# A linear-attention and expert kernel on one core: an early indirect transfer, idle matmuls, one key decay moved, and second loads that wait

## The chip, the cores and the metric

The kernel runs on one core of one Trainium2 chip. The metric is the device time of one execution in microseconds (us); lower is better. The time before is the median of three runs. One further execution was taken with the hardware profiler, and all rows below come from it.

The core's engines run beside each other: PE (TensorE, matrix products; its weight loads are listed as PEld), DVE (VectorE), ACT (ScalarE), POOL (GpSimd) and SP (SyncE), which in this kernel issues nearly all transfers. POOL issues the indirect transfers, whose rows go where a list of numbers says.

## The reference

First a blocked linear attention with decay over q, k and v of shape (4, 8, 768, 64), then a mixture of eight experts of which each token uses one:

```python
for b in range(nb):                                   # 12 blocks of 64 positions
    intra = einsum('bhic,bhjc->bhij', qb, kb) * Dmask
    intra = einsum('bhij,bhjd->bhid', intra, vb)
    inter = einsum('bhid,bhde->bhie', qb * lam_pow, kv_state)
    out[:, :, sl] = intra + inter
    kv_state = lam_block * kv_state + einsum('bhsd,bhse->bhde', kb * rev_pow, vb)
...
x = attention.transpose(0, 2, 1, 3).reshape(3072, 512)
e_idx = argmax(x @ w_gate + modality_bias[modality_id], axis=1)
for e in range(8):
    mask = e_idx == e
    out[mask] = gate_w[mask, None] * (relu(x[mask] @ w1[e]) @ w2[e])
```

## The kernel before

The attention works in blocks of 128 positions: 24 blocks g, six for each of the four batches, two to a load. A pair of blocks is the unit of the main loop (m = 2 to 11); blocks 0 to 5 are written out ahead of it. For each block PE computes `scores(g)` (into a PSUM tile `s`), DVE multiplies them with the decays (`mask`, tile `pt`), PE multiplies with the values (`values`, tile `o`), and adds what comes from the running state (`from_state`, with the decayed queries `qd`, which POOL makes in `query`). `products(g)` multiplies the decayed keys `kd` with the values into PSUM tile `kv`, and `add` on DVE updates the state. The decayed keys are made in `keys`: on ACT in eight pieces (line 238), or on POOL in one instruction (line 234). `give` on ACT copies a finished `o` to `xt`; `turn` and `gates` turn it and compute the gate's logits.

From the middle of the attention on, tokens are sorted: DVE finds the expert and a slot for each token in small steps that `do` releases a few at a time, and POOL writes the rows into a DRAM table `placed` with indirect transfers (`one_slot`, line 433), one after the other, each held by `tick` until a certain matmul is done. After about 100 us the expert tiles follow: twelve wide tiles of 256 rows and two thin ones, each with weights that SP loads into buffers that the tile before has freed.

The order on PE, DVE, ACT and SP is the order of the code. POOL's order is too: `pool` chains its instructions in the order of its calls. Each engine therefore stands still behind an instruction that waits. The pairs of blocks lie in four buffers (`SLOTS`, tag `load`); in the main loop `load(m + SLOTS, [0])` fetches the first block of a later pair and, one pair on, `load(m + SLOTS - 1, [1])` the second block of that buffer.

`decays` and `powers` on DVE (lines 120 and 129) compute the decay tables `dk` and `pq` at the start, and `keep_busy(9)` issues nine bf16 matmuls on zeros, whose result nobody reads, before the first scores.

Of the kernel before, what the change touches and what calls it, by code (L numbers as in the profile page):

```python
# [6 lines left out]
F32 = mybir.dt.float32  # L7
F32R = mybir.dt.float32r
BF16 = mybir.dt.bfloat16
I32 = mybir.dt.int32  # L10
# [5 lines left out]
P = 128  # L16
# [4 lines left out]
SLOTS = 4  # L21
# [22 lines left out]
def linear_attention_moe(tc, qkv, lam, modality, wg, mbias, w1, w2, out):  # L44
    nc = tc.nc
    with ExitStack() as ctx:
        const = ctx.enter_context(tc.tile_pool(name="const", bufs=1))
        dram = ctx.enter_context(tc.tile_pool(name="dram", bufs=1, space=bass.MemoryType.DRAM))
# [12 lines left out]
        def pool(op, free=False):  # L61

            for first in queue[-1:] + ([] if free else loose):
                tc.add_manual_dep(op.ins, first.ins.name,
                                  mybir.DependencyInfo(mybir.DependencyClass.NoSync, mybir.DependencyReason.SCHED_ONLY),
                                  reason="order")
            if free:
                loose.append(op)
            else:
                loose.clear()  # L70
                queue.append(op)
            return op
# [4 lines left out]
        def slot(shape, dt, nm):  # L77

            return work.tile(shape, dt, name=nm, tag="load", bufs=SLOTS)

        def source(m):
            return qkv[divmod(m, NC // HB)].rearrange("x p c f -> p x c f")

        halves = {}

        def load(m, blocks=range(HB)):
            if m not in halves:
                halves[m] = slot([P, 4, HB, H * D], F32, "load")
            last = (HB * m + 1) % NC == NC - 1
            if m > 2 and not last and len(blocks) == HB:  # L90
                nc.sync.dma_start(out=halves[m], in_=source(m))
                return
            for c in blocks:
                for part in ((slice(0, 2), slice(2, 4)) if m < 2 else (slice(0, 4 - (last and c)),)):
                    nc.sync.dma_start(out=halves[m][:, part, c], in_=source(m)[:, part, c])

        for m in range(3):
            load(m)
# [3 lines left out]
        nought = const.tile([P, P], F32, name="nought")  # L102
# [5 lines left out]
        pool(nc.gpsimd.affine_select(out=anti, in_=anti, pattern=[[1, P]], compare_op=ALU.not_equal,  # L108
                                     fill=1.0, base=1 - P, channel_multiplier=1))

        dk = work.tile([P, 2, NP, P], F32, name="dk", bufs=1)
        pq = work.tile([P, NP, P], F32, name="pq", bufs=1)
        lamq = const.tile([P, NP], F32, name="lamq")
# [97 lines left out]
        def loaded(g):  # L211

            t = halves[g // HB][:, :, g % HB]
            kt, qt = (t[:, i].rearrange("p (a t) -> p a t", a=NP) for i in range(2))
            return kt, qt, t[:, 2], t[:, 3]
# [11 lines left out]
        def keys(g, on_pool=False):  # L227

            if g % NC < NC - 1:
                kds[g] = work.tile([P, NP, 2, D], F32, name="kd", bufs=3)  # L230
                kn = loaded(g)[3].rearrange("p (a h d) -> p a h d", a=NP, h=2)
                if on_pool:
                    last = dk[:, :, :, P - 1 : P].rearrange("p h a o -> p a h o").to_broadcast([P, NP, 2, D])
                    pool(nc.gpsimd.tensor_tensor(out=kds[g], in0=kn, in1=last, op=ALU.mult))
                    return
                for p in range(NP):
                    for hl in range(2):
                        nc.scalar.activation(out=kds[g][:, p, hl, :], in_=kn[:, p, hl, :], func=AF.Copy,  # L238
                                             scale=dk[:, hl, p, P - 1 : P])
# [5 lines left out]
        def after(op, mm):  # L245
            tc.add_manual_dep(op.ins, mm.ins.name,
                              mybir.DependencyInfo(mybir.DependencyClass.Sync, mybir.DependencyReason.DATA),
                              reason="order")
            return op

        def scores(g):
            kt, qt, vt, kn = loaded(g)
            scs[g] = ps.tile([P, 2, NP, P], F32, name="s", bufs=2)
            for p in range(NP):
                for hl, r in enumerate(halves2):
                    mm = nc.tensor.matmul(scs[g][:, hl, p, :], kt[r, p, :], qt[r, p, :], start=True, stop=True)  # L256
            begun[g] = mm
            return mm

        def mask(g):  # L260
            pts[g] = work.tile([P, 2, NP, P], F32, name="pt", bufs=4)
            nc.vector.tensor_tensor(out=pts[g], in0=scs.pop(g), in1=dk, op=ALU.mult)  # L262

        def products(g):

            if g % NC < NC - 1:
                vt, kd = loaded(g)[2], kds.pop(g)
                for p in range(NP):
                    for hl, r in enumerate(halves2):
                        nc.tensor.matmul(kp[r, g % HB, p, :], kd[:, p, hl, :],  # L270
                                         vt[:, (2 * p + hl) * D : (2 * p + hl + 1) * D], start=True, stop=True)
# [105 lines left out]
        def gate_rows():  # L377
            lgt = work.tile([P, RC, WG], F32, name="lgt", bufs=2)
            nc.vector.transpose(out=lgt, in_=lps.rearrange("p g (t a) -> p (g t) a", a=Q))
            return lgt  # L380
# [74 lines left out]
        def tick(mm):  # L455

            if jobs:
                after(jobs.pop(0)[1](), mm)
# [347 lines left out]
        def keep_busy(n):  # L806

            nothing = ps.tile([P, NP, P], F32, name="o", bufs=2).rearrange("p a t -> p (a t)")
            for i in range(n):
                nc.tensor.matmul(nothing, busy[:, :P], busy, start=(i == 0), stop=(i == n - 1))  # L810
# [13 lines left out]
        def block(g, on_pool=False):  # L824
            mm = scores(g)
            mask(g)
            keys(g, on_pool)
            query(g)
            return mm
# [5 lines left out]
        keys(0, True)  # L835
        scores(0)
        mask(0)
        scores(1)
        products(0)
        add(0)  # L840
# [1 line left out]
        mask(1)  # L842
        query(1)
        keys(1)
        keys(2)
        from_state((1,))
        values(1)
        scores(2)
# [39 lines left out]
        for m in range(2, pairs):  # L888
            a, b = HB * m, HB * m + 1
            ahead = m + 1 < pairs  # L890
            add(b)
            if m == 4 or m == 8:
                routed = m // 4 - 1, *choose(m // 4 - 1, gate_rows())
            if ahead:
                block(a + 2)
                mm = block(b + 2)
                if m > 4:
                    tick(mm)
                if 2 < m <= pairs - SLOTS:
                    load(m + SLOTS - 1, [1])  # L900
                if m == 9:
                    fetch_w1(*some, parts=range(2, 4))
                elif m == 10:
                    fetch_w2(*some, parts=range(2, 4))
            if m == 5 or m == 9:
                ranks(routed[-1])
                slots += slots_of(*routed)
            if m == 2:
                routing_constants()
            elif m == 3:  # L910
                clear(slice(E * CAP, E * CAP + TT), TT)
            do(9 if m % 4 == 0 else 8)
            if m == 2:
                mm = values(b, begins=True)
                from_state((a, b), ends=True)
            elif not ahead:
                values(a, begins=True)
                mm = values(b, begins=True)
                from_state((a, b), ends=True)
            else:  # L920
                from_state((a, b))
                values(a)
                mm = values(b)
            if m > 4:
                tick(mm)
            if m + SLOTS < pairs:
                load(m + SLOTS, [0])
            if ahead:
                products(a + 2)
                products(b + 2)  # L930
                add(a + 2)
            if m == 10:
                turn_rows(0)
            elif m % 2 and ahead:
                mm = turns(m // 2, begin_list)
                if m == 5 or m == 9:
                    jobs += [("slots", one_slot)] * RC
                if m > 4:
                    tick(mm)
            if m == 8:  # L940
                need("slots")
                raw1 = w1_part("raw1", F32)
                some = fetch_regs(0, True)
                fetch_w1(*some, parts=range(2))
                fetch_x(0)
            elif m == 9:
                raw2 = w2_part("raw2", F32)
                some = fetch_regs(0, True)
                fetch_w2(*some, parts=range(2))
                fetch_x(1)  # L950
# [97 lines left out]
        for n in [3] + list(range(wides, fixed_ones)):  # L1048
# [5 lines left out]
            m = n + 1 if n > 3 else wides  # L1054
# [91 lines left out]
```

## Time and profile before

| what | value |
|---|---|
| median of three runs | 393.74 us (393.1 to 394.73) |
| the profiled execution's own time | 393.09 us |
| its span, first to last instruction | 391.4 us |
| PE busy | 379.1 us (97%) |
| DVE, ACT, POOL busy | 261.2, 211.7, 96.3 us |
| mean granted clock of PE | 0.990 of full |

The profiled execution took 393.09 us, 0.65 us less than the median. 1.7 us of it lie outside the span. Busy time of PE counts matmuls from issue to a modelled end, so a busy PE may still run at half its clock; the granted clock has to be read beside it.

### The profile page before, as it was taken

How to read it: one execution, taken by the hardware profiler on the slowest of the kernel's cores; microseconds unless marked ns; L12 is line 12 of the kernel's file. 1: busy time of each engine (PE TensorE's matmuls, PEld its weight loads, DVE VectorE, ACT ScalarE, POOL GpSimd, SP SyncE). 2: the span in 40 equal slices, each digit the busy share in tenths (PEclk: the TensorE clock that was granted, in tenths of full speed). 3: DMA queues.
4: the chain of work that ended last, by engine and by line, in shares of the span. 5: the costliest groups of instructions: out<-in, count | busy, mean ns of one | idle time of the engine just before them, and what ended most of it. 6: DMA issues, size and time to landing. Idle time of an engine off the chain costs nothing.

```text
span 391.4 us, 9721 instructions
## 1 busy us (share of the span) xinstructions
PE 379.1 (97%) x3597; PEld 337.3 (86%) x3597; DVE 261.2 (67%) x461; ACT 211.7 (54%) x419; POOL 96.3 (25%) x127
## 2 busy tenths in 40 slices
PE   6999999899999999999999999999999999999994
PEld 3888988799888989989898987898979899898983
DVE  6468779988678578886758574376775756667520
ACT  1668578496446464465566444355454644655611
POOL 1365214865520267120010201202011020201112
PEclk9799999999999999999999999999999999999999
DMA  7999986986998994299813999663860211100101
GB/s 249 387 403 359 342 269 214 389 275 165 311 344 266 338 320 160 109 377 340 266 55 77 294 384 346 266 186 91 293 212 36 55 55 44 40 25 10 49 3 52
DMA packets 44568, 82.72 MB, mean 211 GB/s; under 512 B 7390, under 2 KB 20190, under 8 KB 44512
## 3 DMA queue, kind: packets, MB, share of 16 engines
q1 hardware_dynamic: 40592, 69.23, 53.1%
q0 software_dynamic: 3920, 12.78, 8.4%
q8 instruction: 30, 0.49, 0.6%
q14 instruction: 26, 0.21, 0.2%
HBM read 89.52 MB, written 17.84 MB: 274 GB/s over the span
## 4 chain that ended last, share of the span: by engine, by line
PE 39%; issue 33%; DMA 9%; DVE 7%; POOL 6%; ACT 3%; SPq 2%; POOLq 0%; DVEq 0%; ACTq 0%
DMA raw<-in_w_dram 5%; POOL out_dram L736 4%; PE o L692 4%; PE o L694 4%; PE o L693 4%; PE s L256 3%; PE o L313 3%; PE o L332 3%; PE s L694 2%; PE s L693 2%; PE s L692 2%; PE s L712 2%; PE kv L712 2%; DVE pt L262 2%; PE kv L692 2%
## 5 line engine op out<-in xcount | busy, mean ns | idle before, releaser
L601 DVE TENSOR_TENSOR w2l<-raw,w2h 128x1024 fp32r<-128x1024 f32 x48 | 58.8, 1224 | 37.5 <-ACT w2h L600 34.0
L736 POOL DMA_INDIRECT out_dram<-y,idx x24 | 29.6, 1232 | 213.8 <-ACT y L735 171.1
L692 PE MATMUL o<-w2h,hh 128*128 128x512 f32 x192 | 75.3, 392 | 0.0
L694 PE MATMUL o<-w2h,hl 128*128 128x512 f32 x192 | 74.8, 390 | 0.0
L693 PE MATMUL o<-w2l,hh 128*128 128x512 f32 x192 | 74.8, 389 | 0.0
L601 DVE TENSOR_TENSOR w1l<-raw,w1h 128x1024 fp32r<-128x1024 f32 x44 | 51.4, 1220 | 2.0 <-ACT w1h L600 2.0
L600 ACT CAST w2h<-raw 128x1024 fp32r<-128x1024 f32 x48 | 49.9, 1039 | 2.0 <-DMA raw<-in_w_dram 1.9
L692 PE MATMUL kv<-xh,w1h 128*128 128x256 f32 x176 | 49.6, 282 | 0.0
L692 PE MATMUL s<-xh,w1h 128*128 128x256 f32 x176 | 49.6, 282 | 0.0
L693 PE MATMUL s<-xl,w1h 128*128 128x256 f32 x176 | 49.5, 281 | 0.0
L693 PE MATMUL kv<-xl,w1h 128*128 128x256 f32 x176 | 49.5, 281 | 0.0
L694 PE MATMUL s<-xh,w1l 128*128 128x256 f32 x176 | 49.5, 281 | 0.0
L694 PE MATMUL kv<-xh,w1l 128*128 128x256 f32 x176 | 49.4, 281 | 0.0
L692 PEld LDWEIGHTS o<-w2h,hh 128*128 128x128 f32 x192 | 36.1, 188 | 7.9 <-issue 0.8
L600 ACT CAST w1h<-raw 128x1024 fp32r<-128x1024 f32 x44 | 42.8, 1045 | 0.0
L694 PEld LDWEIGHTS o<-w2h,hl 128*128 128x128 f32 x192 | 36.0, 188 | 7.6
L693 PEld LDWEIGHTS o<-w2l,hh 128*128 128x128 f32 x192 | 36.1, 188 | 7.1
L735 ACT ACTIVATE y<-o,idx 128x512 f32<-128x512 f32 x24 | 16.4, 684 | 41.1 <-PE o L694 38.3
L238 ACT ACTIVATE kd<-load,dk 128x64 f32<-128x64 f32 x152 | 37.6, 338 | 0.1
L692 PEld LDWEIGHTS kv<-xh,w1h 128*128 128x128 f32 x176 | 33.3, 189 | 0.4 <-issue 0.4
L692 PEld LDWEIGHTS s<-xh,w1h 128*128 128x128 f32 x176 | 33.2, 189 | 0.3
L693 PEld LDWEIGHTS s<-xl,w1h 128*128 128x128 f32 x176 | 33.2, 189 | 0.4
(190 smaller groups left out, 637.8 us busy)
## 6 DMA issues: line engine op xcount, KB each, us to landing
raw<-in_w_dram SPq DMA_DIRECT2D x96, 512.0 KB
load<-in_qkv_dram SPq DMA_DIRECT2D x12, 1024.0 KB
both<-in_w_dram SPq DMA_DIRECT2D x16, 512.0 KB
xg<-placed SPq DMA_DIRECT2D x48, 128.0 KB
placed<-blank SPq DMA_DIRECT2D x9, 528.0 KB
load<-in_qkv_dram SPq DMA_DIRECT2D x8, 512.0 KB
load<-in_qkv_dram SPq DMA_DIRECT2D x2, 2048.0 KB
load<-in_qkv_dram SPq DMA_DIRECT2D x4, 768.0 KB
```

The costliest lines, as they stand in the source:

```text
L238: nc.scalar.activation(out=kds[g][:, p, hl, :], in_=kn[:, p, hl, :], func=AF.Copy, scale=dk[:, hl, p, P - 1 : P])
L256: mm = nc.tensor.matmul(scs[g][:, hl, p, :], kt[r, p, :], qt[r, p, :], start=True, stop=True)
L313: mm = nc.tensor.matmul(op[place(g, hl), p, :], vt[:, (2 * p + hl) * D : (2 * p + hl + 1) * D], pt[:, hl, p, :], start=((begins or g % NC ...
L332: nc.tensor.transpose(out=tp[:, p, :], in_=xts[grp][:, p, tb].rearrange("k t a -> k (t a)"), identity=ident)
L600: nc.scalar.copy(out=hi, in_=src)
L601: nc.vector.tensor_tensor(out=lo, in0=src, in1=hi.bitcast(F32), op=ALU.subtract)
L692: nc.tensor.matmul(out, ah, bh, start=first, stop=False)
L693: nc.tensor.matmul(out, ah, bl, start=False, stop=False)
L694: return nc.tensor.matmul(out, al, bh, start=False, stop=last)
L712: mm = nc.tensor.matmul(hp[:, j, :], raw1[i][:, kc, fs], xt2[:, kc, :], start=(kc == 0), stop=(kc == KC - 1))
L735: nc.scalar.activation(out=y, in_=yp, func=AF.Copy, scale=idx[:, t, 1:2].bitcast(F32))
L736: sc = nc.gpsimd.indirect_dma_start(out=out, out_offset=bass.IndirectOffsetOnAxis(ap=idx[:, t, 0:1], axis=0), in_=y, in_offset=None, bound ...
```

## The change

Four edits:

1. Near the start, POOL gets an `iota` (the numbers 0 to 127, tile `each`) and an indirect transfer of 128 rows of 16 zeros to a DRAM scratch `unread` that nothing reads. Both stand in POOL's order behind the constant `anti` and ahead of the first decayed keys.
2. `keep_busy(7)`: seven more matmuls on zeros between the scores of block 0 and those of block 1.
3. `keys(2, True)`: the decayed keys of block 2 are made by POOL in one instruction, not by ACT in eight.
4. `load` returns its transfer, and for m = 3 to 8 the load of the second block waits until `mm`, the last matmul of the scores of block b + 2, is done (`after`).

```diff
@@ load @@
             if m > 2 and not last and len(blocks) == HB:
-                nc.sync.dma_start(out=halves[m], in_=source(m))
-                return
+                return nc.sync.dma_start(out=halves[m], in_=source(m))
             for c in blocks:
                 for part in ((slice(0, 2), slice(2, 4)) if m < 2 else (slice(0, 4 - (last and c)),)):
-                    nc.sync.dma_start(out=halves[m][:, part, c], in_=source(m)[:, part, c])
+                    op = nc.sync.dma_start(out=halves[m][:, part, c], in_=source(m)[:, part, c])
+            return op
@@ constants @@
+        each = const.tile([P, 1], I32, name="each")
+        pool(nc.gpsimd.iota(each, pattern=[[0, 1]], base=0, channel_multiplier=1))
+        unread = dram.tile([P, 16], F32, name="unread")
+        pool(nc.gpsimd.indirect_dma_start(out=unread, out_offset=bass.IndirectOffsetOnAxis(ap=each, axis=0),
+                                          in_=nought[:, :16], in_offset=None))
@@ blocks 0 to 3 @@
         scores(0)
         mask(0)
+        keep_busy(7)
         scores(1)
@@
         keys(1)
-        keys(2)
+        keys(2, True)
         from_state((1,))
@@ main loop @@
                 if 2 < m <= pairs - SLOTS:
-                    load(m + SLOTS - 1, [1])
+                    after(load(m + SLOTS - 1, [1]), mm)
```

The order of PE's instructions, before, from the first scores on (`s` is a scores tile, `load_70` the buffer of blocks 0 and 1, `load_75` that of blocks 2 and 3):

```order
L256 MATMUL s_165<-load_70 128x128 x8
L256 MATMUL s_176<-load_70 128x128 x8
L270 MATMUL kv_124<-load_70,kd_163 64x64 x8
L313 MATMUL o_194<-pt_174,load_70 64x128 x8
L303 MATMUL o_227<-qd_207,state1_122 64x128 x8
```

and in the change, at the same place (the first row is scores(0) again, and the weight load and matmul on `busy` stand there seven times):

```order
L261 MATMUL s_169<-load_70 128x128 x8
L815 LDWEIGHTS busy_83
L815 MATMUL o_180<-busy_83 128x512
...
L261 MATMUL s_188<-load_70 128x128 x8
L275 MATMUL kv_128<-load_70,kd_167 64x64 x8
L318 MATMUL o_206<-pt_178,load_70 64x128 x8
```

The idle matmuls stand between the scores of block 0 and those of block 1; behind them the order is as it was, five line numbers on.

The order of POOL's instructions, before, from the constant `anti` on:

```order
L108 AFFINE_SELECT anti_89<-anti_89 128x128
L234 TENSOR_TENSOR kd_163<-load_70,dk_94 128x512
L223 TENSOR_TENSOR qd_207<-load_70,pq_95 128x512
L223 TENSOR_TENSOR qd_256<-load_75,pq_95 128x512
L223 TENSOR_TENSOR qd_283<-load_75,pq_95 128x512
L157 MEMSET ident_114 128x128
```

and in the change:

```order
L108 AFFINE_SELECT anti_89<-anti_89 128x128
L112 IOTA each_94 128x1
L114 DMA unread_96<-nought_85,each_94 128x16
L239 TENSOR_TENSOR kd_167<-load_70,dk_98 128x512
L228 TENSOR_TENSOR qd_219<-load_70,pq_99 128x512
L239 TENSOR_TENSOR kd_230<-load_75,dk_98 128x512
L228 TENSOR_TENSOR qd_261<-load_75,pq_99 128x512
L228 TENSOR_TENSOR qd_288<-load_75,pq_99 128x512
L162 MEMSET ident_118 128x128
```

The indirect transfer stands ahead of the keys of block 0, and the keys of block 2 (`kd_230`) between the queries of blocks 1 and 2.

## Rows read from the trace of the kernel before

**Rows 1.** The profile's page: its head and the busy time of each engine (us, share, instructions).

```profile
span 391.4 us, 9721 instructions
PE 379.1 (97%) x3597; PEld 337.3 (86%) x3597; DVE 261.2 (67%) x461; ACT 211.7 (54%) x419; POOL 96.3 (25%) x127
```

**Rows 2.** Waits of PE: us in total, times, longest.

```profile
PE s L256 <- DMA load<-in_qkv_dram: 2.3, 2, 1.7
PE o L332 <- DVE grp L336: 1.3, 1, 1.3
```

**Rows 3.** Stretches, expert stage: busy us of each engine, granted clock, DMA share, GB/s.

```profile
300.00:320.00 20.00, 20.00 (x127) 18.12 (x126) 13.42 (x15) 10.82 (x14) 2.57 (x2) 1.00 0.15 41
```

**Rows 4.** Timeline of PE's matmuls: start, length (us), line, tiles, count [idle before].

```profile
1.29 3.69 PE L810 MATMUL o<-busy 128*128 128x512 bf16 x9 [1.29 <-DVE busy L101]
5.56 1.16 PE L256 MATMUL s<-load 64*128 64x128 f32 x16 [0.58 <-DMA load<-in_qkv_dram]
8.47 2.08 PE L256 MATMUL s<-load 64*128 64x128 f32 x16 [1.75 <-DMA load<-in_qkv_dram]
...
14.98 1.09 PE L313 MATMUL o<-pt,load 128*64 128x128 f32 x16
...
16.00 1.16 PE L256 MATMUL s<-load 64*128 64x128 f32 x16
...
17.09 0.69 PE L270 MATMUL kv<-load,kd 128*64 128x64 f32 x16
...
22.13 1.10 PE L303 MATMUL o<-qd,state 64*64 64x128 f32 x32
```

**Rows 5.** Stretches of the start; the third last number is the granted clock.

```profile
8.00:9.00 1.00, 0.53 (x4) 0.54 (x6) 1.00 (x3) 0.00 (x0) 0.27 (x1) 0.50 1.05 401
10.00:20.00 10.00, 9.57 (x138) 8.32 (x138) 4.35 (x8) 6.65 (x26) 3.58 (x3) 0.76 1.05 387
```

**Rows 6.** The start on POOL, DVE and ACT: timeline, and the powers' line by itself.

```profile
7.21 1.06 POOL L234 TENSOR_TENSOR kd<-load,dk 128x512 f32<-128x512 f32 x1 [5.81 <-DMA load<-in_qkv_dram]
8.79 1.19 DVE L262 TENSOR_TENSOR pt<-s,dk 128x1024 f32<-128x1024 f32 x1
13.83 3.93 ACT L238 ACTIVATE kd<-load,dk 128x64 f32<-128x64 f32 x16
L129 DVE TENSOR_TENSOR_SCAN pq<-lamq,nought x4: 393/412/1260, 6.6 to 8.5; 128x128 f32<-128x128 f32 x4
```

**Rows 7.** POOL's first indirect transfer: its waits in 58.4 to 60, then timeline.

```profile
L433 POOLq EVENT_SEMAPHORE  x2: 43/68/94, 58.5 to 58.6; - x2
64.25 1.19 POOL L433 DMA_INDIRECT placed<-grp,sloti  x1 [9.30 <-DVE sumsEA L374]
65.47 2.49 POOL L223 TENSOR_TENSOR qd<-load,pq 128x512 f32<-128x512 f32 x2
```

**Rows 8.** DVE and PE behind that transfer: timeline.

```profile
64.73 3.29 DVE L374 TENSOR_TENSOR pastA<-pastA,deltaA 128x16 f32<-128x16 f32 x1
68.55 1.09 PE L303 MATMUL o<-qd,state 64*64 64x128 f32 x28 [0.82 <-DVE state L280]
71.93 1.51 DVE L374 TENSOR_TENSOR atA<-atA,sidx 128x2 f32<-128x2 f32 x1
75.65 1.23 PE L332 MATMUL o<-ident,xt 128*128 128x128 f32 x8 [1.31 <-DVE grp L336]
```

**Rows 9.** Two stretches inside that wait; the last two numbers are DMA share and GB/s.

```profile
61.00:62.00 1.00, 1.00 (x20) 0.88 (x19) 1.00 (x2) 1.00 (x5) 0.00 (x0) 1.00 1.05 385
63.00:64.00 1.00, 1.00 (x24) 1.00 (x21) 0.93 (x4) 1.00 (x6) 0.00 (x0) 1.00 0.00 0
```

**Rows 10.** Timeline of PE: the scores of blocks 8 and 9, 12 and 13, 14 and 15.

```profile
35.37 2.06 PE L256 MATMUL s<-load 64*128 64x128 f32 x32
...
49.64 2.06 PE L256 MATMUL s<-load 64*128 64x128 f32 x32
...
59.48 2.06 PE L256 MATMUL s<-load 64*128 64x128 f32 x32
```

## The prediction, made before the changed kernel ran

> **What bounds the kernel now.** I read the page's head first: PE is busy 97% of a span of 391.4 us [rows 1]. The reader should see that little idle time is left, so the next view is the list of PE's waits. It is short: 2.3 us in two waits for the first loads, 1.3 us for a copy on DVE [rows 2], then 0.8 us for the state on DVE [rows 8]; nothing else on it is above 0.8 us but the start. In the expert stage PE has no idle time (20.00 of 20 us at clock 1.00) [rows 3] and the others are far below it, so what PE gains in the attention should arrive at the end, unless a load or a copy is then late.
>
> Busy time hides one thing, the clock. Eight score products of one block (16 records) take 1.16 us at 5.56 and again at 16.00, but 2.08 us at 8.47 [rows 4]. Ahead of 8.47 PE had waited 1.75 us for a load, and 0.58 us before that. The granted clock is 0.50 at 8 to 9 us, the level of 1.2 GHz, and 0.76 in the mean of 10 to 20 us [rows 5], so it is half until (1 - 0.76) x 10 / 0.5 = 4.8 us into that stretch, about 14.8. So there are two places where PE loses time that this change touches: the start, and the region of 64 to 76 us where the two waits for DVE lie [rows 8].
>
> **The second place first (edit 1).** POOL's first indirect transfer had its last waits at 58.5 and 58.6, yet it begins at 64.25 [rows 7]: 5.65 us in which it waits for nothing that shows. No later one does this. I read it as a cost of first use. What hangs on it: POOL makes the decayed queries of two blocks only at 65.47, for 2.49 us [rows 7]. Meanwhile DVE runs a tiny step of the list, which takes 3.29 us from 64.73, as long as POOL's instruction lasts; the same again at 71.93, 1.51 us [rows 8]. Behind these stand the state update and the row copies, and PE waits 0.82 and 1.31 us for them [rows 8]. If the first use is paid at 1.6 us, this transfer goes out at 58.6, the queries are made from about 60.5 (they need the scores at 59.5 to 61.5 [rows 10]), and are over at 63, before DVE comes to its small steps. Gain 0.82 + 1.31 = 2.1 us. Its bounds are 0 (the steps meet another POOL instruction) and 2.4 (the small waits of 0.2 us nearby go too).
>
> The Trainium skill (GPSIMD Engine Reference, section 2.1) says that the first call of a freshly loaded kernel pays some 6 us (5.95 us measured there) that no instruction in a profile shows. The row's 5.65 us agrees; by the page's figure the sum below would be 0.3 us smaller, as the first keys would come that much later.
>
> **The first use in its new place.** It begins at about 1.6 us, behind `anti`, and by the row's 5.65 us and 1.19 us for the transfer itself POOL is free at 8.5. The keys of block 0 (1.06 us, at 7.21 before [rows 6]) then end at 9.55, not 8.27. That costs nothing if the products of block 0 could not start before about 9.5; they come behind the scores of block 1, which start with their load at 8.47, whatever the clock. It even gives something: beside those keys one of DVE's power steps took 1260 ns, where the shortest takes 393 [rows 6]. Without that, `mask(0)`, at 8.79 before, starts at about 7.95 and ends at 9.15.
>
> **Edit 2, the idle matmuls.** At the start nine of them take 3.69 us, 0.41 each [rows 4], nearly all at the lower level, judging by what the same scores take before and after. At full clock I estimate half, 0.21 each, so seven take 1.5 us from 6.72 to 8.2: they end before the load at 8.47 and leave 0.25 us of the gap. Whether the clock then holds no row tells; bounds: it falls as before (gain 0), or holds throughout. The nearest row for holding is the wait of 1.31 us at 75.65 [rows 8], through which the clock stayed at 1.00. I take that it holds.
>
> Then PE's path, with one block's scores at 1.0, products at 0.55, values at 0.95, state at 1.0 us (rows at full clock less the 0.1 by which neighbours overlap [rows 4]), and loads at the 387 GB/s of this stretch [rows 5], that is 1.36 us for each half of a block after 8.47: block 2's halves at 11.2 and 12.5, block 3's at 13.9 and 15.3, block 4 at 18.0, block 5 at 20, blocks 6 and 7 at 25.8, blocks 8 and 9 at 31.2.
> - scores(1) 8.47 to 9.5; products(0) 9.6 to 10.15 (keys at 9.55); values(0) to 11.1; DVE copies the state to 10.7 and masks block 1 to 11.9; from_state(1) to 12.1; values(1) to 13.05.
> - ACT gives block 0 at 11.15 to 11.7 and makes the keys of block 1 in 8 x 0.246 us (3.93 for 16 [rows 6]) to 13.7. scores(2) to 14.05, products(1) to 14.6, scores(3) to 15.6 (its load 13.9).
> - products(2) to 16.15: its keys, now on POOL, were made at 12.5 to 13.6. values(2) to 17.1. DVE masks block 3 at 17.35, so values(3) ends at 18.3; the keys of block 3 wait for their half load at 15.3 and end at 17.3; products(3) to 18.85; from_state(2, 3) to 19.9.
>
> Before, that last step ended at 22.13 + 1.10 = 23.2 [rows 4]. Gain 3.3 us by this walk; I take 3.0, since each handover costs some tens of ns that it leaves out. The following scores need loads that land at 18 to 31.2, and blocks 8 and 9 were computed at 35.37 [rows 10], 32.4 then, so 1.2 us of slack is left at the tightest.
>
> **Edit 3.** By the same walk ACT would have had the keys of block 2 at 15.65, about when PE wants them, and those of block 3 at 18.2. So POOL's instruction is worth 0 to 0.3 us with the clock up; I take nothing by itself. It lies in POOL's idle time between two queries. If that cover were gone it would cost its 1.06 us. The Trainium skill (GPSIMD Engine Reference, section 1) speaks against it: GpSimd and VectorE contend for SBUF when a VectorE instruction has two SBUF inputs. The 1260 ns and the 3.29 us rows agree with that rule. By the walk DVE has only a masked product from PSUM or nothing at 12.5 to 13.6, so the sum is the same by either.
>
> **Edit 4.** Six second loads wait for scores(2m + 3), and SP's queue with them. Behind each in SP's order stands a first load that waits for later values anyway. The block concerned is read by scores(2m + 7): for m = 3 the wait ends at 37.4 and the reader starts block 12 at 49.64 [rows 10], some 13 us later; the other five have as much. A block of 1.05 MB takes 2.7 us, and 2.7 more behind the one ahead. I cost it at nothing; uncovered it would be a few us for each load.
>
> **The sum.** 393.09 (the profiled execution) - 2.1 - 3.0 = 388.0. The median stood 0.65 above that execution, so 388.6.
>
> **The rivals.**
> - *The first use comes again* at 58 us, because the code did not stay through the fills, iotas and selects between. For it: those operations lie only there, never between two indirect transfers of the trace. Against it: products and copies do lie between, at no cost. It gives 393.74 - 3.0 = 390.7.
> - *The clock falls all the same*, or the idle matmuls run at the lower level (seven at 0.41 end at 9.6, 1.1 us after the load) and give back what they win. It gives 393.74 - 2.1 = 391.6. The Trainium skill (TensorE: Matmul & The Clock Gate, Part 1) says that the activity window runs free of the kernel's start, so the level changes elsewhere from run to run; no single trace shows that.
> - *Nothing arrives*: the gain is given back where a load or ACT is late. Against it: 1.2 us of slack at the tightest load, and ACT and DVE move with PE. It gives 393.7.
> - *Slower*: the first use is drawn out at the start. For it: at 61 to 62 us the DMA share was 1.05, at 63 to 64 it was 0.00 [rows 9], and the transfer began right after; if the first use had waited for quiet transfers, it would find none early, where the share is 1.05 [rows 5]. Each us beyond the 5.65 delays keys(0) and all of PE. All gain (5.1) is gone at 10.8 us, and at 12.8 us the kernel is 2 us slower; at 17, 400. Against it: 5.65 us is close to a fixed cost, and the loads are not yet at full rate at 1.6 us.
>
> **How the numbers follow.** A measurement of this kernel can tell about 0.5%, 2.0 us, from no change. Chances: both gains 0.60 (387.2 to 390), first use again 0.13 (390.7), clock falls 0.13 (391.6), nothing arrives 0.08, slower 0.06. The likeliest gives 388.6, with bounds 387.2 (2.4 + 3.3 and half a us of spread between runs) and 390 if half of one gain is lost. The two partial cases belong to the 8 in 10, so the range is 387.0 to 391.9. Faster by over 0.5% is below 391.77: 0.60, nearly all of the second case and about half of the third, 0.79. Same: 0.15. Slower: 0.06.
>
> **What would show it.** In the new profile: a transfer on POOL that begins near 7 us and none at 58 to 64 that is late; the granted clock at 1.00 from 8 to 15 us and scores(1) in 1.16 us; the scores of block 4 at about 20, of blocks 18 and 19 some 5 us earlier; no waits of PE of 0.8 and 1.3 us near 64 to 72; the expert stage without idle time. Wrong it would be if keys(0) came after 10 us, if the clock fell near 8 us, or if PE waited for `load` between 20 and 60 us.

## The result, and the profile after

The changed kernel took 390.07 us (median of 6 runs, 389.89 to 391.61); the kernel before, beside it, 393.99 us (6 runs, 393.1 to 394.73). The ratio is 0.9908 [0.9886, 0.993]: faster by 0.9%. The profiled execution took 390.03 us against 393.09 before, 3.06 us less (3.92 in the medians); 5.1 were forecast. The forecast of 388.6 was right in its direction and the time lies in its range, 1.5 us above the middle.

The page of the changed kernel: head, busy time, and PE's longest waits.

```profile
span 388.3 us, 9736 instructions
...
PE 378.6 (97%) x3604; PEld 336.0 (87%) x3604; DVE 257.3 (66%) x461; ACT 209.8 (54%) x411; POOL 99.5 (26%) x130
```

```profile
...
PE o L337 <- ACT xt L297: 1.2, 2, 0.7
...
PE s L261 <- DMA load<-in_qkv_dram: 0.3, 1, 0.3
```

The two waits of [rows 8] and the 2.3 us for the first loads [rows 2] are gone; the wait for a copy on ACT, 0.8 us before in two waits of which the longest took 0.5, has grown to 1.2 and 0.7. The timeline of the changed kernel, at the start, in the region of the second place, and at the end:

```profile
2.27 1.14 POOL L114 DMA_INDIRECT unread<-nought,each  x1 [0.78 <-POOL each L112]
...
5.66 1.57 PE L261 MATMUL s<-load 64*128 64x128 f32 x16 [0.34 <-DMA load<-in_qkv_dram]
...
7.16 1.69 PE L815 MATMUL o<-busy 128*128 128x512 bf16 x7
7.33 1.21 POOL L239 TENSOR_TENSOR kd<-load,dk 128x512 f32<-128x512 f32 x1 [3.91 <-DMA load<-in_qkv_dram]
8.74 1.19 DVE L267 TENSOR_TENSOR pt<-s,dk 128x1024 f32<-128x1024 f32 x1
8.77 1.16 PE L261 MATMUL s<-load 64*128 64x128 f32 x16
...
19.53 1.10 PE L308 MATMUL o<-qd,state 64*64 64x128 f32 x32
20.56 1.16 PE L261 MATMUL s<-load 64*128 64x128 f32 x16
...
56.87 1.05 POOL L438 DMA_INDIRECT placed<-grp,sloti  x1 [4.50 <-PE o L337]
56.88 2.06 PE L261 MATMUL s<-load 64*128 64x128 f32 x32
...
62.71 1.12 PE L261 MATMUL s<-load 64*128 64x128 f32 x13
...
64.06 1.40 PE L261 MATMUL s<-load 64*128 64x128 f32 x19 [0.22 <-issue]
...
64.45 1.62 DVE L285 SCALAR_TENSOR_TENSOR state<-state,pq,kv 128x64 f32<-128x64 f32 x8 [1.94 <-remote]
...
69.55 1.09 PE L337 MATMUL o<-ident,xt 128*128 128x128 f32 x8 [0.69 <-ACT xt L297]
...
72.60 2.06 PE L261 MATMUL s<-load 64*128 64x128 f32 x32
...
96.17 1.99 PE L717 MATMUL s<-xt,raw 128*128 128x256 f32 x8
...
383.95 0.98 POOL L789 DMA_INDIRECT out_dram<-yn,to  x1 [1.33 <-ACT yn L788]
```

The same places in the trace of the kernel before (the scores of blocks 18 and 19, the first expert matmul, the last transfer):

```profile
76.80 2.06 PE L256 MATMUL s<-load 64*128 64x128 f32 x32
...
100.05 2.21 PE L712 MATMUL s<-xt,raw 128*128 128x256 f32 x9
...
387.14 0.99 POOL L784 DMA_INDIRECT out_dram<-yn,to  x1 [0.66 <-ACT yn L783]
```

And the stretches of the changed kernel (columns as in [rows 5]), with the wait of the first transfer to `placed`:

```profile
8.00:9.00 1.00, 1.00 (x8) 0.42 (x8) 1.00 (x2) 0.00 (x0) 0.54 (x1) 1.00 1.07 414
10.00:20.00 10.00, 9.57 (x192) 8.63 (x195) 5.80 (x14) 4.99 (x18) 6.87 (x14) 1.00 1.05 390
300.00:320.00 20.00, 20.00 (x127) 18.12 (x126) 13.00 (x15) 11.38 (x16) 2.56 (x2) 1.00 0.20 54
```

```profile
L438 POOLq EVENT_SEMAPHORE  x2: 43/70/96, 55.9 to 56.0; - x2
```

What the reader is to see:

- **The start.** The granted clock is 1.00 at 8 to 9 us and over 10 to 20, and the second scores take 1.16 us where they took 2.08 [rows 4]. The step that ended before at 23.2 ends at 20.63: 2.6 us won. The scores of block 0 took 1.57 us here and 1.16 before, and the idle matmuls begin at 7.16 and end at 8.85, so the second scores begin at 8.77, some 0.3 us behind the landing of their load.
- **The second place.** The first transfer to `placed` begins 0.87 us behind its last wait, not 5.65 [rows 7]. The scores of blocks 14 and 15 are 2.60 us earlier than in [rows 10]. Those of blocks 18 and 19 stood at 76.80 in the trace of before and are at 72.60, 4.20 earlier: this place gave 1.6.
- **The early transfer** waits 0.78 us, and the first keys come at 7.33, when their load lands, 0.12 later than in [rows 6]. Nothing of 5.65 us is paid there.
- **What is given back.** The first expert matmul is at 96.17, before at 100.05 (3.88 earlier); the last transfer starts at 383.95, before at 387.14 (3.19 earlier). So 0.3 us is lost near 95 us and 0.7 in the tail, behind PE's last matmul.

### The profile page after: what moved, and what is told of

It reads as the page before. It is cut to its first block, busy times and chain, and to the rows that moved or that the text cites. A ratio compares the mean times of both kernels' runs of the same rounds, so it can differ in the third digit from the quotient of the medians.

```text
span 388.3 us, 9736 instructions
## 1 busy us (share of the span) xinstructions
PE 378.6 (97%) x3604; PEld 336.0 (87%) x3604; DVE 257.3 (66%) x461; ACT 209.8 (54%) x411; POOL 99.5 (26%) x130
## 4 chain that ended last, share of the span: by engine, by line
PE 44%; issue 33%; DMA 9%; POOL 7%; ACT 3%; DVE 2%; SPq 1%; POOLq 0%; DVEq 0%; ACTq 0%
PE s L261 5%; PE o L318 4%; POOL out_dram L741 4%; PE o L697 4%; PE o L698 4%; PE o L699 4%; DMA xg<-placed 4%; PE o L337 3%; PE o L308 2%; DMA both<-in_w_dram 2%; PE s L699 2%; PE s L698 2%; PE s L697 2%; PE s L717 2%; PE kv L717 2%
## 5 line engine op out<-in xcount | busy, mean ns | idle before, releaser
L243 ACT ACTIVATE kd<-load,dk 128x64 f32<-128x64 f32 x144 | 35.7, 337 | 1.6 <-DMA load<-in_qkv_dram 1.5
L438 POOL DMA_INDIRECT placed<-grp,sloti x24 | 27.1, 1130 | 25.2 <-PE o L337 10.0
```

Of the source, the lines that this page charges most:

```text
L438: sc = nc.gpsimd.indirect_dma_start(out=placed, out_offset=bass.IndirectOffsetOnAxis(ap=at, axis=0), in_=row, in_offset=None)
```

## The experiments

Three theories on the late transfer were set against each other. FIRST USE: the transfer pays a fixed price the first time, wherever it stands (the prediction's reading). LOADS: it waits until the loads in flight are through. PLACE: the stop belongs to a fixed place in POOL's stream of instructions, and two more ahead move the stop to another place, away from the transfer. No kernel here leaves out or changes any of the reference's computation.

The experiments ran on three chips, so a time is compared with the kernel before on the same chip: 390.38 us (24 runs, 388.62 to 393.47) in the first, 390.31 (31 runs, 388.63 to 393.29) in the second, 392.49 (30 runs, 391.04 to 395.76) in the third.

### The first chip: each edit undone

**Without the early transfer:**

```diff
-        each = const.tile([P, 1], I32, name="each")
-        pool(nc.gpsimd.iota(each, ...))
-        unread = dram.tile([P, 16], F32, name="unread")
-        pool(nc.gpsimd.indirect_dma_start(out=unread, ...))
```

> The changed kernel without its early indirect transfer and its list of numbers (edit 1 undone); the other three edits stay. Theory FIRST USE (the first indirect transfer pays once, wherever it stands): the first transfer to the table of placed rows is late again by about 5 us behind its last wait, PE waits near 63 to 72 us come back, the kernel is about 1.6 us slower than the changed one (about 391.7). Rival LOADS (the transfer waited for loads in flight, and holding the second loads back cleared its way): the transfer begins within 1 us of its last wait all the same, and the time stays near 390.1. Rival PLACE (a fixed place in POOL's instruction stream stalls, whatever stands there): as FIRST USE here.

Measured: 387.91 us (387.6 to 388.15), ratio 0.9917 [0.9886, 0.9948]. The first transfer to `placed` begins at 59.02, 2.8 us behind its last wait at 56.2. So it is late again, by half of what it was, and that costs next to nothing: the scores of blocks 18 and 19 follow those of 14 and 15 at 14.97 us (14.57 in the three other kernels on this chip, where it is not late). That the kernel would be slower, as FIRST USE had it, and that the transfer would be on time, as LOADS had it, are both wrong here; the late transfer is as PLACE had it, and in this kernel one more instruction than before (the keys of block 2) stands ahead of it. The start of PE, timeline:

```profile
5.59 1.16 PE L256 MATMUL s<-load 64*128 64x128 f32 x16 [0.39 <-DMA load<-in_qkv_dram]
6.68 1.68 PE L810 MATMUL o<-busy 128*128 128x512 bf16 x7
8.55 1.16 PE L256 MATMUL s<-load 64*128 64x128 f32 x16 [0.19 <-DMA load<-in_qkv_dram]
```

**Without the idle matmuls:**

```diff
-        keep_busy(7)
```

> The changed kernel without the seven idle matmuls (edit 2 undone). If the idle matmuls hold the clock and that is worth what the trace shows (the scores of block 4 come 2.6 us earlier), the granted clock falls to half near 8 us again and the kernel is 2.0 to 2.6 us slower (392.1 to 392.7). Rival: the gain of the start came from the quicker power steps and from the moved keys, and the kernel stays within 0.5 us of 390.1.

Measured: median 387.91 us, but 387.55 to 391.05; 7 of 12 lie within 387.55 to 387.99 and 5 at 389.1 to 391.05; ratio 0.9951 [0.9922, 0.9979]. Its profiled execution (389.1) is one of the five; timeline of PE and stretches:

```profile
8.64 2.08 PE L261 MATMUL s<-load 64*128 64x128 f32 x16 [1.77 <-DMA load<-in_qkv_dram]
...
21.93 1.16 PE L261 MATMUL s<-load 64*128 64x128 f32 x16
```

```profile
8.00:9.00 1.00, 0.35 (x2) 0.35 (x4) 1.00 (x2) 0.00 (x0) 0.61 (x1) 0.77 1.05 406
10.00:20.00 10.00, 9.57 (x163) 8.48 (x162) 5.45 (x13) 4.89 (x18) 5.73 (x9) 0.90 1.05 389
```

The clock falls, for less of the stretch than before (0.90 against 0.76 [rows 5]), and the scores of block 4 come at 21.93, about 1.5 us later than in the two other kernels on this chip that make the keys of block 2 on POOL (20.34 and 20.38). The median is not 2.0 to 2.6 us slower, as was expected, but two of the five late runs, 390.5 and 391.05, have a mean granted clock of 0.989 and 0.988, and no other run here lies below 0.995.

**Keys of block 2 on ACT again:**

```diff
-        keys(2, True)
+        keys(2)
```

> The changed kernel with the keys of block 2 on ACT again (edit 3 undone). By the walk in the prediction ACT is done with them about when PE wants them: 0 to 0.5 us slower (390.1 to 390.6). Rival: ACT becomes the bound of the start, since block 3's keys come behind them: 1 us or more slower.

Measured: 387.97 us (387.67 to 390.0), ratio 0.9928 [0.9895, 0.9961]. The scores of block 4 follow those of block 1 by 11.79 us, as in the changed kernel (20.56 - 8.77): nothing on the path. Three of the nine runs lie at 388.7 to 390.0, at a mean granted clock of 0.997 to 0.999; what made them longer is open.

**The second loads not held back:**

```diff
-                    after(load(m + SLOTS - 1, [1]), mm)
+                    load(m + SLOTS - 1, [1])
```

> The changed kernel without the wait of the second loads (edit 4 undone). FIRST USE: no late transfer at 56 to 58 us, time within 0.5 us of the changed kernel. LOADS: the first transfer to the table is late again by some 5 us, and the kernel about 1.6 us slower (391.7).

Measured: 387.80 us (387.47 to 387.99), ratio 0.9924 [0.9897, 0.995]. The transfer begins 0.85 us behind its wait although the loads go on (DMA share 1.06 at 56 to 57 us): LOADS alone is against this.

### The second chip: both kernels again, and two edits alone

**Before, unchanged, and after, unchanged:**

> The kernel before, unchanged, for a profile beside the others on one chip. In its profile the first transfer to the table of placed rows is some 5 us late (FIRST USE and PLACE), or late by the length of the loads in flight (LOADS); the clock falls to half near 8 us.

> The changed kernel, unchanged, on the same chip: 0.6 to 1.2% faster than the kernel before. The four kernels with one edit undone all stood at 387.8 to 388.0 beside 390.4 for the kernel before; if the edits are worth what the first pair of traces shows, this one is at least 1.5 us faster than those without the transfer or the idle matmuls (386.4 or less by the same scale); if they overlap, it stands at 387.9 like the rest.

Measured: 390.46 us (388.59 to 393.54) and 387.83 us (387.51 to 388.05, 8 runs), ratios 0.9998 and 0.9923 [0.9897, 0.995]. The kernel before scatters over 5 us, the changed one over 0.5. The changed kernel stands at 387.83, like those with one edit undone: the edits overlap. In the changed kernel the scores of blocks 18 and 19 follow those of 14 and 15 at 14.57 us, without the stops near 63 us; in the kernel before at 17.58. So on this chip the second place is worth 3.0 us. The kernel before, stretches, then timeline, around its late transfer (last wait at 58.7):

```profile
61.00:62.00 1.00, 1.00 (x20) 0.88 (x18) 1.00 (x3) 1.00 (x6) 0.00 (x0) 1.00 1.05 387
62.00:63.00 1.00, 1.00 (x21) 0.83 (x18) 1.00 (x2) 1.00 (x6) 0.00 (x0) 1.00 0.46 158
63.00:64.00 1.00, 1.00 (x24) 1.00 (x21) 0.97 (x3) 1.00 (x5) 0.00 (x0) 1.00 0.00 0
```

```profile
64.52 1.19 POOL L433 DMA_INDIRECT placed<-grp,sloti  x1 [9.45 <-ACT kd L238]
```

**Edit 4 alone** (on the kernel before):

```diff
-                    load(m + SLOTS - 1, [1])
+                    after(load(m + SLOTS - 1, [1]), mm)
```

> The kernel before with edit 4 alone (the second loads wait). LOADS: the first transfer to the table begins within 1.5 us of its last wait and the kernel is 1.5 to 2.4 us faster than before. FIRST USE: the transfer is as late as in the kernel before and the time within 0.5 us of it.

Measured: 389.67 us (387.86 to 391.64), ratio 0.9968 [0.9939, 0.9998]. The transfer's waits end at 55.7, the loads go quiet near 56.6, and it begins at 58.91, as these stretches and this row of the timeline show:

```profile
56.00:57.00 1.00, 1.00 (x12) 0.83 (x12) 0.74 (x2) 0.74 (x3) 0.00 (x0) 1.00 0.63 236
57.00:58.00 1.00, 1.00 (x22) 1.00 (x20) 1.00 (x4) 0.98 (x5) 0.00 (x0) 1.00 0.00 0
```

```profile
8.48 1.16 PE L256 MATMUL s<-load 64*128 64x128 f32 x16 [1.21 <-DMA load<-in_qkv_dram]
...
58.91 1.19 POOL L433 DMA_INDIRECT placed<-grp,sloti  x1 [6.84 <-ACT kd L238]
```

With POOL's stream as before, then, the lateness does follow the loads: it ends some 2 us after they go quiet, and holding them back shortens it from 5.8 to 3.2 us. Neither forecast is met: the transfer does not begin within 1.5 us of its wait, and it is not as late as before. The first row is a second find: in this execution the clock did not fall at the start, without any idle matmul.

**Edit 1 alone** (the block of edit 1 added to the kernel before):

> The kernel before with edit 1 alone (the early indirect transfer). FIRST USE: the transfer to the table is no longer late and the kernel 1.6 to 2.4 us faster than before. LOADS: late as before, time within 0.5 us of it.

Measured: 388.11 us (387.41 to 390.85), ratio 0.9953 [0.993, 0.9976]. Its waits end at 55.8; stretch and timeline:

```profile
56.00:57.00 1.00, 1.00 (x13) 0.83 (x13) 0.72 (x2) 0.72 (x3) 0.40 (x1) 1.00 1.06 408
```

```profile
56.60 1.05 POOL L438 DMA_INDIRECT placed<-grp,sloti  x1 [4.51 <-PE o L337]
```

The transfer goes out 0.8 us behind its wait, under full traffic (DMA share 1.06). With POOL's stream moved by two instructions the loads do not hold it up. The median is 2.2 us below that of the kernel before, as FIRST USE had it; PLACE would have it so too.

### The third chip: FIRST USE against PLACE

**Idle matmuls alone** (on the kernel before):

```diff
+        keep_busy(7)
```

> The kernel before with edit 2 alone (seven idle matmuls). Theory: the idle matmuls take away the runs in which the clock is low in the first 15 us, and nothing else. Then the runs lie close together, the scores of block 14 come at about 57 us as in the changed kernel, but the first transfer to the table is late by 3 to 6 us, so the kernel stands about where the kernel before has its fastest runs (388.6), 1.5 to 2 us below its median. Rival: the clock is worth nothing in most runs; then the median stays within 0.5 us of the kernel before.

Measured: 391.47 us (391.12 to 393.77; 9 of 12 within 391.1 to 391.75), ratio 0.9986 [0.9958, 1.0014]. The scores of blocks 14 and 15 come at 56.72, but the transfer is late as before: waits to 55.9, start 61.45. The median is 1.0 us below the kernel before, between the two forecasts, and the interval does not tell it from no change.

```profile
61.45 1.19 POOL L433 DMA_INDIRECT placed<-grp,sloti  x1 [9.25 <-DVE sumsEA L374]
```

**Three plain instructions, no early transfer** (on the kernel before):

```diff
+        each = const.tile([P, 1], I32, name="each")
+        pool(nc.gpsimd.iota(each, ...))
+        pool(nc.gpsimd.iota(each, ...))
+        pool(nc.gpsimd.iota(each, ...))
```

> The kernel before with three plain number lists on POOL in the place of the early transfer (none of the other edits). PLACE (a place in POOL's instruction stream stalls): as with the transfer alone, the first transfer to the table begins within 1 us of its last wait and the median is near 388.1. FIRST USE: it is late until the loads in flight are through, as in the kernel before, and the median is near 390.3.

Measured: 391.27 us (389.61 to 394.41), ratio 0.9985 [0.9958, 1.0012]. The time alone tells nothing: six of the 12 runs have a mean granted clock of 0.988 to 0.993. The trace, that of the fastest run, does (semaphores, timeline, stretch):

```profile
L437 POOLq EVENT_SEMAPHORE  x2: 43/69/95, 55.6 to 55.7; - x2
```

```profile
5.45 1.37 PE L260 MATMUL s<-load 64*128 64x128 f32 x16
...
8.44 1.16 PE L260 MATMUL s<-load 64*128 64x128 f32 x16 [1.63 <-DMA load<-in_qkv_dram]
...
56.66 1.20 POOL L437 DMA_INDIRECT placed<-grp,sloti  x1 [4.62 <-PE o L336]
...
63.85 1.22 PE L260 MATMUL s<-load 64*128 64x128 f32 x17 [0.23 <-issue]
```

```profile
57.00:58.00 1.00, 1.00 (x22) 1.00 (x20) 1.00 (x4) 0.97 (x5) 0.86 (x1) 1.00 1.05 406
```

This transfer is the first indirect one of the whole program, the loads run at a share of 1.05, and it is not late. FIRST USE falls with this one run.

**The early transfer moved behind the first keys** (in the changed kernel, its block now stands between `keys(0, True)` and `scores(0)`):

> The changed kernel with the early transfer moved behind the keys of block 0, to about 8.5 us, where the loads already keep the DMA engines full (share 1.05) and do so until about 48 us. FIRST USE WITH FIXED PRICE (5.65 us): it begins at about 14.2 us, the queries of block 1 are 4 to 5 us late, the kernel 3.5 to 5 us slower than the changed one. FIRST USE BEHIND THE TRAFFIC (it is over 2 us after the loads have gone quiet): POOL stands until the loads let it through, up to some 50 us, and the kernel is 10 us or more slower. LOADS or PLACE: no more than 1.3 us slower.

Measured: 391.24 us (391.02 to 393.13), ratio 0.9974 [0.9946, 1.0002]. Timeline:

```profile
8.92 1.17 POOL L839 DMA_INDIRECT unread<-nought,each  x1 [0.29 <-DVE pq L129]
...
57.09 1.05 POOL L433 DMA_INDIRECT placed<-grp,sloti  x1 [4.51 <-PE o L332]
...
64.30 1.50 PE L256 MATMUL s<-load 64*128 64x128 f32 x22 [0.20 <-issue]
```

The first use waits 0.29 us among loads at full rate. A price behind the traffic is out too. But the time is not what LOADS or PLACE had: the ratio of 0.9974 beside the changed kernel's 0.9923 on the second chip is some 2 us, not 1.3 or less. The stop at 64 us (last row) is part of it; the rest is open, and the changed kernel itself was not run on this chip.

**Fewer idle matmuls, and block 13's keys on POOL** (in the changed kernel):

```diff
-        keep_busy(7)
+        keep_busy(5)
...
-                mm = block(b + 2)
+                mm = block(b + 2, m == 5)
```

> The changed kernel with five idle matmuls in place of seven and the keys of block 13 on POOL. The scores of block 1 then start with their load (0.3 us earlier) and PE's wait of 0.5 us for ACT near 53 us goes: 387.0 to 387.3 where the changed kernel has 387.8. Rival: five do not hold the clock, and some runs lie 1.5 to 3 us higher.

Measured: 388.49 us (388.46 to 390.63, 7 runs), ratio 0.9908 [0.9873, 0.9944]. PE's wait for ACT of 0.53 us near 53 us in the changed kernel is gone, and the scores of blocks 14 and 15 come at 56.37. It was not run beside the changed kernel, and its ratio of 0.9908 is the one that the changed kernel had in the result, so whether it is better isn't settled.

## Why the prediction was right, and where it was not

- **Edit 1: the gain is real, the reading failed.** The step is "I read it as a cost of first use". The table shows the first transfer to `placed` in eight of the 14 traces:

| POOL's instructions ahead, kernel | last wait, start | late by, us | early transfer | 8 KB packet begins |
|---|---|---|---|---|
| as before: before | 58.6, 64.25 | 5.65 | no | 62.07 |
| as before: before again | 58.7, 64.52 | 5.8 | no | 62.33 |
| as before: idle matmuls alone | 55.9, 61.45 | 5.6 | no | 59.27 |
| as before: edit 4 alone | 55.7, 58.91 | 3.2 | no | 56.87 |
| one more: without the early transfer | 56.2, 59.02 | 2.8 | no | 56.84 |
| two more: edit 1 alone | 55.8, 56.60 | 0.8 | yes | 52.58 |
| three more: plain instructions | 55.7, 56.66 | 1.0 | no | 52.56 |
| three more: after | 56.0, 56.87 | 0.87 | yes | 51.76 |

In the six traces that are not listed two to four more stand ahead, and the transfer is 0.84 or 0.85 us late. What divides the traces is the number of instructions ahead, not whether an indirect transfer was made: up to one more it is late, from two more on it is not. Where it is late, the start follows the end of the loads. So POOL's queue stood at a fixed place between the waits and the transfer, until loads in flight were through. PLACE is shown. That the gain of edit 1 came all the same is luck: it came by two instructions more in the stream, which need not have been a transfer.

The traces point to an owner too. Instructions are themselves fetched by the DMA engines, and the page of the kernel before has a queue for them whose packets hold 8 KB each (packets, MB, share):

```profile
q14 instruction: 26, 0.21, 0.2%
```

The last column of the table is the start of that queue's packet nearest ahead of the transfer. In the five late traces it begins at the end of the loads, and the transfer follows 2.04 to 2.19 us later, whatever the lateness; in the others it begins ahead of the last wait, where POOL waits anyway. Between the kernel before and the one with three plain instructions nothing but POOL's stream has changed, and the packet has moved from behind the waits to ahead of them. These views of the DMA queues show it, before at 62.0 to 62.5 us, then with the plain instructions at 52.5 to 53.0 us:

```profile
q14 instruction: 1, 0.01, 4.1%
```

```profile
q14 instruction: 1, 0.01, 3.9%
```

So the stop is a fetch of POOL's next instructions, stuck behind the loads, as far as timing can show it: the rows of the queue don't name the engine that a packet is for.

The Trainium skill (Runtime: NRT & Kernel Launch, section Instruction fetch mechanics) says that instructions come in blocks of 16 KiB through a DMA queue of the sequencer's own, and that crossing a block's end is mostly hidden. The packets here are 8 KB, 0.21 MB in 26; behind loads at a share of 1.05 the 2.8 to 5.8 us of the table were not hidden, and ahead of the last wait they were.

- **The price of 5.65 us in the new place.** The same error: it was 0.78 us, so the first keys were at 7.33 and not 8.5. The power step beside them still took 1217 ns (1260 in [rows 6]), and `mask(0)` began at 8.74, not 7.95. By the figure of the Trainium skill (GPSIMD Engine Reference, section 2.1) that the prediction set beside its row, the early transfer would have waited some 6 us; the 0.78 and 0.29 us measured decide against it for this kind of transfer. With it falls the rival "slower", which rested on the same price.
- **Size of edit 1.** 2.1 was forecast, 1.6 came in the pair of traces, since PE and DVE stopped near 63 us for what the profile lists as "issue" and "remote", and PE waited 0.69 for ACT. Where these stops don't occur it is 3.0 (14.57 against 17.58): the term was too small, not too large.
- **Edit 2: the clock held, but the size is that of one execution.** The clock stayed at 1.00, and the start gave 2.6 us of the 3.0. The step that was short is the idle matmuls' end, "from 6.72 to 8.2": they ended at 8.85, behind scores of block 0 that took 1.57 us. A larger error is that the kernel before doesn't lose this much in every run. The clock record of each trace tells when the granted clock first rose to full; the scores of block 0 (1.16 us at full clock) are longer where it rose late:

| kernel | idle matmuls | clock rose, us | scores of block 0, us | gap ahead of block 1, us | scores of block 1, us |
|---|---|---|---|---|---|
| before | no | 4.51 | 1.16 | 1.75 | 2.08 |
| before again | no | 4.66 | 1.16 | 1.80 | 2.08 |
| without the idle matmuls | no | 5.12 | 1.16 | 1.77 | 2.08 |
| plain instructions | no | 5.91 | 1.37 | 1.63 | 1.16 |
| edit 4 alone | no | 6.76 | 1.72 | 1.21 | 1.16 |
| edit 1 alone | no | 7.28 | 1.98 | 1.00 | 1.16 |
| without the early transfer | yes | 4.96 | 1.16 | 0.19 | 1.16 |
| after | yes | 6.55 | 1.57 | none | 1.16 |

Without idle matmuls the clock fell in the three traces where it had risen early, and held in the three where it rose late. In the changed kernel's own trace it rose late, so that it held there doesn't show what the idle matmuls do: part of the 2.6 us is the luck of that pair. What shows it is the kernel without the early transfer, where it rose at 4.96 and held, and the runs: of 85 of the kernel before on the three chips 25 have a mean granted clock below 0.993, and all but one of these are longer than their chip's median; of 61 with seven idle matmuls none has. So the idle matmuls take away the runs in which the clock falls, and in the median, where it mostly doesn't, they are worth some 0 to 1 us (0.1 on the first chip, 387.91 against 387.80 without edit 4; 1.0 on the third). They don't make every run as good: in two kernels that have them and lack other edits the times still reach 390.0 and 393.77 at a clock of 0.997. The prediction named a clock that moves from run to run, in a rival, and then added 0.65 us for the median as if each run lost the same. The Trainium skill (TensorE: Matmul & The Clock Gate, Part 1), which says that the window runs free of the kernel's start, agrees with the rise at 4.51 to 7.28 us behind matmuls that began at 1.29.
- **Edit 3 at nothing: right** (387.97 against 387.83 and the same 11.79 us).
- **Edit 4 at nothing: right in the sum, wrong alone.** With edit 1 there it gives nothing (387.80 without it, 387.83 with it, on two chips whose kernels before stood at 390.38 and 390.31). Alone it gives 0.3% [0.0, 0.6], by the shorter lateness of the old stream. Edits 1 and 4 meet at one stall, so undoing either alone cost 0.4 us at most there. The loads it holds back are not missed: PE waits 0.3 us for loads in all.
- **The expert stage has no idle time**, as forecast, but some of the gain is lost ahead of it and behind: 4.20 at 72.6 us, 3.88 at 96.2, 3.19 at the last transfer. The extra stops near 63 us are in the trace of after in the result and, on the third chip, in those of the plain instructions and of the moved transfer; they are not in that of after on the second chip, whose profiled execution is 2.2 us shorter (387.83 against 390.03), nor in that with five idle matmuls on the third. What makes them is open; no run was made for it.
- **The range.** Its lower bound of 387.2 comes out at 387.5 from its own terms (393.74 - 2.4 - 3.3 - 0.5); nothing else rests on it.

In sum: 5.1 forecast, 3.06 between the profiled executions: 0.4 short at the start, 0.5 short at the second place, 1.1 given back later.

## What to carry to other kernels

A wait that shows no owner and happens once need not belong to the instruction behind it: put a few plain instructions ahead, see whether it moves, and whether a packet of an instruction queue begins shortly ahead of its end, before paying for a warm-up of that instruction. Undoing one edit at a time hides a gain that two edits reach by different ways; run each alone too. Where a loss depends on a clock that differs from run to run, size it from the scatter of many runs, not from one profile.

## What the runs showed of the hardware

- GpSimd's queue can stop for 2.8 to 5.8 us between two instructions while loads fill the DMA engines (share 1.05), and go on some 2 us after they end; an 8 KB packet on an instruction queue begins 2.04 to 2.19 us ahead of the late transfer. Two instructions more ahead took the stop away from there.
- A first indirect transfer cost no extra wait above 0.78 us, at 2.27 us or, among full traffic, at 8.92 us.
- TensorE's granted clock first rose to full at 4.51 to 7.28 us in 14 traces whose matmuls begin at the same place. Without idle matmuls a gap of 1.75 to 1.80 us behind an early rise (4.51 to 5.12 us) let it fall to 0.50; one of 1.00 to 1.63 us behind a late rise (5.91 to 7.28 us) didn't.
